# Chunk bounds in four groups over eight places of the array, with the selection turned in 64-column pieces

## The chip, the cores and the metric

The kernel runs on one core of one Trainium2 chip. The metric is the device time of one execution in microseconds (us); the median of the runs stands for a kernel. Names of engines: PE is TensorE (matmuls), ACT is ScalarE, DVE is VectorE, POOL is GpSimd, SP issues most DMAs.

## The reference

Two parts, one after the other. The first is causal attention over 4 batches of 8 heads, 768 positions and 64 dimensions, in which each query sees only 6 of 24 chunks of 32 keys: those with the highest upper bound of the score. The second is a feed-forward block over the 3072 rows of 512 that result.

```python
k_min = np.min(k_chunks, axis=3)
k_max = np.max(k_chunks, axis=3)
ub = np.sum(np.maximum(q[:, :, :, None, :] * k_min[:, :, None, :, :], q[:, :, :, None, :] * k_max[:, :, None, :, :]), axis=-1)
ub = np.where(causal, ub, -1000000000.0)
top_chunks = np.argsort(ub, axis=-1)[..., -top_k:]
scores = scale * np.matmul(q, k.transpose(0, 1, 3, 2))
mask = sel & (pos[:, None] >= pos[None, :])
scores = np.where(mask, scores, -1000000000.0)
attn = softmax(scores); return np.matmul(attn, v)
...
xn = x / rms * rms_g
return (silu(xn @ w_gate) * (xn @ w_val)) @ w_out
```

(The two softmax and silu lines are shortened; the reference writes them out.)

## The kernel before

The work is cut into steps. Each step has the engines that may run it, a modelled duration, a rank, the steps it needs, and the buffers that it opens or uses. Before any instruction is issued, the class `Order` plays the steps through: each engine takes, among the steps that are ready and whose buffers are free, the one with the lowest rank. The steps are then emitted in that order, so this plan fixes the order of the instructions of each engine. A rank is a sum of keys: a time for the place (`a5` for the preparation of pair 5, `l5` for its loads, `s5.0` for its scores, `f1.0` for the first half of batch 1's feed-forward, from the table `TIMES`), an offset for the kind of step in the first or in a later batch (table `RANK`), and a pace times the number of the step.

Attention works in 16 pairs of heads, four to a batch. The preparation of a pair (`prep`) is this chain:

- k and q are loaded by SP and turned by PE (L499) into tiles `kt` and `qt` with two heads of 64 dimensions on 128 partitions and 768 columns; ACT or DVE copies them out of PSUM.
- DVE takes minima and maxima of each chunk (L523, L525). Their difference is the second half of `ku`, and `rt` is the positive part of q, so that the bound is q times the minimum plus rt times the difference.
- PE makes the bounds (L578), as small float32 matmuls: 64 rows (one head) by 32 columns (the chunks) at a place of their own in the array, over 256 queries. There are three groups of 256 queries on three of the four column places, and two heads on the two halves of rows: six places.
- The two results of 96 partitions by 256 columns are copied to `ubs` by ACT or DVE, and turned by PE into `up` (L602, four turns), with queries on the partitions.
- DVE adds the causal mask `cmf` (L610), takes the eight largest of each row (L623, 12 instructions) and compares with the sixth (L631, L636). The result `selq` holds for each of 6 blocks of 128 queries two heads of 64 columns.
- PE turns `selq` into `st` (L647, six turns of 128 by 128), and two copies, one to each head (L315 on ACT, L319 on DVE), bring it into the rows of the operand `qs` that q does not use.

The scores (L712) are matmuls of `ke` with `qs`: 64 rows are k and q, the others a fixed matrix `e_all` and the selection, which adds a large negative number where a chunk is not selected. The rows in use are 89 for one head and 128 for the other. ACT takes the exponential (L729), PE multiplies by v (L748), DVE divides and writes the rows `xb` (L763, L764). Pair 3 is scored in two halves of the queries (`s3.0` and `s3.3`), the others whole.

The feed-forward block runs in halves of a batch, 384 rows each. The rows are normalised and turned (L830); then come 12 steps of gate (L864) and value (L885) matmuls, tanh and two products on ACT and DVE, and the projection (L905) with its store. The feed-forward half `f0.0` needs the first three row blocks of all four pairs of batch 0; the half `f0.1` the other three.

The PSUM banks are eight (`ps`), with limits for each use; three sets of score operands (`set`), two buffers of rows (`xb`).

Of the kernel before, what the change touches and what calls it, by code (L numbers as in the profile page):

```python
# [8 lines left out]
FP32 = mybir.dt.float32  # L9
# [18 lines left out]
        av=-17.99, dif=13.38, eps=15.18, exp=27.56, kC=-0.16, kE=17.53, kT=-23.78, kload=11.87,  # L28
        kmn=22.63, kmx=-12.26, max=-61.12, qC=54.11, qE=9.45, qT=-26.18, qload=3.56,
        relu=19.97, root=46.9, sc=-0.2, sel=-44.38, selC=-65.79, selT=-14.62, sq=17.6, tp=7.31,  # L30
        tpE=23.87, ub=-8.14, ubE=18.31, ubm=-7.93, up=-18.76, vload=-10.11, xb=16.97, xs=25.31,
    ),
    dict(
        av=-15.37, dif=-18.4, eps=-17.61, exp=10.72, gate=-5.25, hh=-22.22, kC=13.17, kE=-4.98,
        kT=-1.03, kload=0.17, kmn=-41.84, kmx=7.41, mask=-29.68, max=20.31, out=-9.4, po=2.14,
        poE=-2.1, qC=3.39, qE=-3.84, qT=-9.81, qload=-3.16, relu=-0.35, root=5.16, sc=-14.52,
        sel=-54.35, selC=-24.54, selT=7.81, sq=37.75, tanh=-21.52, tg=-0.17, tp=-45.38,
        tpE=12.9, ub=-13.71, ubE=24.1, ubm=13.82, up=-10.31, val=1.94, vload=19.85, xb=5.4,
        xs=11.14,
# [3 lines left out]
TIMES = dict(  # L43
    pace0=1.79, pace1=0.05, pacen=0.06, step=0.1, w=-2.85, w0=-2.54, w1=11.0, w2=43.12,
    w3=21.59,
)
for p, x in enumerate((
    13.52, 22.61, 22.24, 36.48, 50.85, 112.1, 73.87, -93.04, 37.77, 179.84, 214.26, 206.91,
    226.56, 220.49, 246.48, 309.33,
)):  # L50
    TIMES[f"a{p}"] = x
for p, x in enumerate((
    -126.16, -42.1, -31.16, -25.49, -5.8, -2.4, 25.7, 37.05, 124.03, 155.87, 181.98, 170.69,
    131.44, 202.23, 282.06, 292.24,
)):
    TIMES[f"l{p}"] = x
for p, x in enumerate((
    -21.19, 10.14, 25.24, 47.31, 25.73, 45.99, 41.69, 141.19, 75.77, 129.26, 185.37, 166.25,
    277.81, 251.34, 143.95, 194.34,
)):  # L60
    TIMES[f"s{p}.0"] = x
for p, x in enumerate((
    101.79,
), 3):
    TIMES[f"s{p}.3"] = x
for i, x in enumerate((
    -27.88, 91.19, 93.6, 105.43, 90.44, 106.14, 282.0, 341.37,
)):
    TIMES[f"n{i // 2}.{i % 2}"] = x
for i, x in enumerate((  # L70
    50.8, 120.12, 121.42, 191.74, 229.9, 291.93, 266.48, 339.66,
)):
    TIMES[f"f{i // 2}.{i % 2}"] = x
for i, x in enumerate((
    2.53, 0.58, 0.91, 2.16, 0.75, 2.5, 0.51, 0.73,
)):
    TIMES[f"pacef{i // 2}.{i % 2}"] = x

# [141 lines left out]
def kernel(  # L224
# [24 lines left out]
    KM = D + NCH + 1  # L249
    W = S // 2  # L250
    G = 3
# [82 lines left out]
    SELQ = [const.tile([P, NT, 2, D], BF16, name=f"selq{i}") for i in range(SLOTS["selq"])]  # L334
    VX = [const.tile([P, 2 * NT, D + 1], BF16, name=f"vx{i}") for i in range(SLOTS["vext"])]
    e_all = const.tile([D, S], BF16, name="e_all")
    cmf = const.tile([P, NT, 2, NCH], FP32, name="cmf")
# [9 lines left out]
    def make_ident(e):  # L347
# [13 lines left out]
        VX[i][:, :, D:D + 1], 1.0)) for i in range(SLOTS["vext"])]  # L361

    def e_step(n):
        if n == 0:
            nc.gpsimd.memset(e_all[:], -BIGE)
        elif n == 1:
            nc.gpsimd.affine_select(
                out=e_all[:], in_=e_all[:], compare_op=ALU.is_ge, fill=0.0,
                base=0, pattern=[[1, S]], channel_multiplier=-CH,
            )  # L370
        elif n == 2:
            nc.gpsimd.affine_select(
                out=e_all[:], in_=e_all[:], compare_op=ALU.is_ge, fill=0.0,
                base=CH - 1, pattern=[[-1, S]], channel_multiplier=CH,
            )
        else:

            nc.gpsimd.affine_select(
                out=e_all[:], in_=e_all[:], compare_op=ALU.not_equal, fill=-1.0,
                base=-NCH, pattern=[[0, S]], channel_multiplier=1,  # L380
            )
# [4 lines left out]
    c_e = prev  # L386
# [11 lines left out]
    def make_cmf(n):  # L398
        if n == 0:
            nc.gpsimd.memset(cmf[:], 0.0)  # L400
        for g4 in (2 * n, 2 * n + 1):
            nc.gpsimd.affine_select(
                out=cmf[32 * g4:32 * (g4 + 1)], in_=cmf[32 * g4:32 * (g4 + 1)],
                compare_op=ALU.is_ge, fill=-BIGC,
                base=g4, pattern=[[4, NT], [0, 2], [-1, NCH]], channel_multiplier=0,
            )

    c_cm = add("cmf", "POOL", 1.5, -70, lambda e: make_cmf(0), [c_e])
    c_cm = add("cmf", "POOL", 1.1, -69, lambda e: make_cmf(1), [c_cm])

# [60 lines left out]
    def prep(c, i0, nb, at, lr):  # L471
# [96 lines left out]
        nj = nq // P  # L568
# [3 lines left out]
        def bounds(e):  # L572
            t = [tile_of(x, [P, 2 * P], FP32, "ub") for x in ub]
            for m, src in ((0, big["q"].tile), (1, rel.tile)):
                for g in range(G):
                    for h in range(2):
                        rows = slice(h * D, (h + 1) * D)
                        nc.tensor.matmul(  # L578
                            t[h][g * CH:(g + 1) * CH, 0:nq], KU[c.ku.slot][rows, m, :],
                            src[rows, g * nq:(g + 1) * nq],  # L580
                            start=(m == 0), stop=(m == 1), tile_position=(h * D, g * CH))

        um = add("ub", "PE", 0.25 + 0.8 * nq / 256, rank(at, b, "ub"), bounds,
# [3 lines left out]
        for h in range(2):  # L587
            def ub_out(e, h=h):
                if ubs.tile is None:
                    tile_of(ubs, [G * CH, 2, 2 * P], FP32, "ubs")  # L590
                evict(e, ubs.tile[:, h, 0:nq], ub[h].tile[0:G * CH, 0:nq])

            ue.append(add("ubE", "", {e: {"ACT": act(nq), "DVE": dve(nq)}[e] for e in BOUNDS},
                          rank(at, b, "ubE", h, "step"), ub_out, [um], opens=[ubs],
                          uses=[ub[h]]))
        up, ubm, m8 = Buf("ps", "prep"), Buf("ubm"), Buf("small")

        def up_turn(e):
            t = tile_of(up, [P, G, nj, 2, CH], FP32, "up")
            for j in range(nj):  # L600
                for h in range(2):
                    nc.tensor.transpose(  # L602
                        t[:, :, j, 1 - h, :], ubs.tile[:, h, j * P:(j + 1) * P],
                        ident_f[0:G * CH, 0:G * CH])

        ut = add("up", "PE", 0.083 * 2 * nj, rank(at, b, "up"), up_turn, ue, opens=[up], uses=[ubs])

        def causal(e):
            t = tile_of(ubm, [P, NT, 2, NCH], FP32, "ubm")
            nc.vector.tensor_tensor(  # L610
                out=t[:, 0:nb].rearrange("p i h c -> p (i h) c"),
                in0=up.tile[:].rearrange("p g j h c -> p (g j h) c")[:, :, 0:NCH],
                in1=cmf[:, i0:i0 + nb].rearrange("p i h c -> p (i h) c"), op=ALU.add)
# [3 lines left out]
        for j in range(0, nb, 3):  # L617
            def top(e, j=j):
                if m8.tile is None:
                    tile_of(m8, [P, NT, 2, 8], FP32, "m8")  # L620
                for x in range(j, j + 3):
                    for h in range(2):
                        nc.vector.max(out=m8.tile[:, x, h, :], in_=ubm.tile[:, x, h, :])  # L623
# [4 lines left out]
        def pick(e):  # L628
            s12 = SELQ[sq.slot][:, 0:nb].rearrange("p i h e -> p (i h) e")
            m12 = m8.tile[:, 0:nb].rearrange("p i h e -> p (i h) e")  # L630
            nc.vector.scalar_tensor_tensor(  # L631
                out=s12[:, :, 0:NCH],
                in0=m12[:, :, 5:6].to_broadcast([P, 2 * nb, NCH]),
                scalar=THRFLOOR, in1=ubm.tile[:, 0:nb].rearrange("p i h e -> p (i h) e"),
                op0=ALU.max, op1=ALU.is_gt)
            nc.vector.tensor_scalar(  # L636
                out=s12[:, :, NCH:NCH + 1], in0=m12[:, :, 0:1], scalar1=-GUARD,
# [6 lines left out]
        def sel_turn(e):  # L644
            t = tile_of(st, [P, nb * P], BF16, "st")
            for j in range(nb):
                nc.tensor.transpose(  # L647
                    t[:, j * P:(j + 1) * P], SELQ[sq.slot][:, j].rearrange("p h c -> p (h c)"),
                    ident_b[:])

        sT = add("selT", "PE", nb * 0.057, rank(at, b, "selT"), sel_turn, [pk, c_idb], opens=[st], uses=[sq])
        fin = []
        for hl, rows in ((0, slice(D, P)), (1, slice(0, D))):
            def sel_out(e, hl=hl, rows=rows):
                evict(e, QS[c.set.slot][hl][rows, cols], st.tile[rows, :])

            fin.append(add("selC", "", {"DVE": dve(n / 2), "ACT": act(n)},
                           rank(at, b, "selC", hl, "step"), sel_out, [sT],
# [28 lines left out]
    def scores(c, i0, nb, at, pace, adds):  # L687
# [3 lines left out]
        for hl in range(2):  # L691
            kk = slice(0, KM) if hl == 0 else slice(0, P)
# [4 lines left out]
            for g, (nd, regions) in enumerate(groups):  # L697
# [25 lines left out]
                need = list(c.sel) + [y for z in c.ke.values() for y in z] + [c_tri] + c_ke  # L723
# [244 lines left out]
```

## Time and profile before

| what | value |
|---|---|
| median of 3 runs | 330.02 us (328.67 to 330.77) |
| span of the profiled execution | 461.2 us |
| mean granted TensorE clock in it | 0.663 |
| busy: PE, DVE, ACT, POOL | 446.6, 246.5, 214.3, 118.0 us |
| moved by DMA | 27.89 MB, mean 60 GB/s |

The profiled execution is known by its span alone: no time outside the span is recorded for it. It was taken at a lower granted TensorE clock than full speed, and it is longer than each of the runs in the first row. A busy PE is one with a matmul under way; matmuls overlap, and their ends are modelled. Rows of the profile name line, engine, operation, written and read tiles, shapes and count, then busy time and the mean duration of one instruction in ns, then the idle time of the engine before them with what ended it. Rows of the timeline begin with the start and the duration in us, from the first instruction to the last of those merged.

### The profile page before, as it was taken

What the parts mean: (1) busy time and instruction counts of PE and PEld (TensorE: products, weight loads), DVE (VectorE), ACT (ScalarE), POOL (GpSimd) and SP (SyncE); (2) the same over time, 40 slices, a digit from 0 to 9 for tenths busy, and PEclk for the clock granted to TensorE, in tenths of its full rate; (3) what the DMA queues carried; (4) which work ended last, traced back from release to release, by engine and by line L of the source; (5) the groups of instructions that cost most, each with busy time, mean ns of one, the idle gap of its engine ahead of it and who ended that gap; (6) DMA issues with size and microseconds to landing.
All of it is one profiled execution on the core that took longest, in us unless ns stands there. A gap on an engine that the chain in (4) does not pass through costs nothing.

```text
span 461.2 us, 7853 instructions
## 1 busy us (share of the span) xinstructions
PE 446.6 (97%) x2978; PEld 253.4 (55%) x2996; DVE 246.5 (53%) x663; ACT 214.3 (46%) x448; POOL 118.0 (26%) x172
## 2 busy tenths in 40 slices
PE   3999999999999999999999999999999999999996
PEld 2677754665666555435666664654565644534442
DVE  2977776665465735404767564367046465603520
ACT  3777772463556643114656684630473634123201
POOL 7755342314442420002552453200110110000000
PEclk9666666666666666666666666666666666666666
DMA  9999769248848250003430203100100000011002
GB/s 186 210 207 143 104 105 100 41 47 53 185 89 134 18 112 9 0 30 105 111 36 1 18 2 46 41 1 1 47 24 0 2 0 1 1 63 52 0 0 91
DMA packets 82645, 27.89 MB, mean 60 GB/s; under 512 B 75568, under 2 KB 79408, under 8 KB 82608
## 3 DMA queue, kind: packets, MB, share of 16 engines
q1 hardware_dynamic: 52528, 19.14, 17.9%
q0 software_dynamic: 28512, 7.87, 17.3%
q10 hardware_dynamic: 1568, 0.39, 0.5%
q8 instruction: 23, 0.38, 0.3%
q14 instruction: 14, 0.11, 0.1%
HBM read 28.57 MB, written 6.29 MB: 76 GB/s over the span
## 4 chain that ended last, share of the span: by engine, by line
PE 96%; DMA 2%; ACT 1%; issue 1%; ACTq 0%
PE vp L885 20%; PE gp L864 20%; PE po L905 20%; PE sc L712 12%; PE av L748 6%; PE ub L578 5%; PE pk L499 3%; PE pq L499 3%; PE tp L830 2%; PE up L602 2%; PE st L647 2%; DMA knat<-in_k_dram 1%; PE sc L718 1%; DMA qnat<-in_q_dram 1%; ACT pt L729 0%
## 5 line engine op out<-in xcount | busy, mean ns | idle before, releaser
L885 PE MATMUL vp<-xT,wv 128*128 128x384 bf16 x384 | 107.5, 430 | 0.0
L864 PE MATMUL gp<-xT,wg 128*128 128x384 bf16 x384 | 107.3, 430 | 0.0
L729 ACT ACTIVATE pt<-sc 128x512 bf16<-128x512 f32 x192 | 91.1, 551 | 20.5 <-PE sc L712 16.6
L905 PE MATMUL po<-wo,hh 128*128 128x512 bf16 x274 | 97.8, 513 | 1.9 <-issue 0.8
L871 ACT ACTIVATE sg<-gp 128x384 bf16<-128x384 f32 x96 | 47.1, 491 | 88.9 <-PE gp L864 78.9
L877 DVE SCALAR_TENSOR_TENSOR tg<-sg,gp 128x384 bf16<-128x384 bf16 x96 | 52.5, 550 | 52.2 <-ACT sg L871 51.4
L893 DVE TENSOR_TENSOR hh<-vp,tg 128x384 bf16<-128x384 f32 x96 | 53.1, 555 | 38.1 <-PE vp L885 37.9
L712 PE MATMUL sc<-qs,ke 89*128 89x128 bf16 (+5 forms) x416 | 72.1, 309 | 0.4 <-PE sc L712 0.2
L885 PEld LDWEIGHTS <-wv 128*128 128x128 bf16 x384 | 45.3, 120 | 43.7 <-issue 3.4
L864 PEld LDWEIGHTS <-wg 128*128 128x128 bf16 x384 | 45.1, 120 | 41.4 <-issue 2.5
L905 PEld LDWEIGHTS <-hh 128*128 128x128 bf16 x288 | 33.5, 120 | 46.8 <-issue 43.8
L735 POOL TENSOR_SCALAR_AFFINE_SELECT pt<-pt 128x512 bf16<-128x512 bf16 (+1 forms) x48 | 24.8, 532 | 102.1 <-ACT pt L729 100.5
L748 PEld LDWEIGHTS <-pt 128*128 128x128 bf16 x672 | 39.1, 111 | 16.5 <-issue 8.2
L712 PEld LDWEIGHTS <-ke 89*128 89x128 bf16 (+1 forms) x420 | 38.2, 116 | 16.0 <-issue 8.6
L748 PE MATMUL av<-vx,pt 128*128 128x65 bf16 x672 | 45.2, 217 | 0.3 <-ACT pt L729 0.2
L317 ACT ACTIVATE osb<-po 128x512 f32<-128x512 f32 x23 | 13.7, 597 | 64.5 <-PE po L905 64.5
L319 POOL CAST ke<-kt 64x768 bf16<-64x768 f32 x31 | 26.1, 843 | 61.0 <-ACT kt L315 57.5
L319 POOL CAST qs<-qt 64x768 bf16<-64x768 f32 x31 | 29.0, 936 | 49.1 <-ACT qt L315 32.5
L499 PE MATMUL pq<-ident_f,qnat 128*128 128x128 f32 x96 | 20.4, 358 | 5.2 <-DMA qnat<-in_q_dram 5.2
L499 PE MATMUL pk<-ident_f,knat 128*128 128x128 f32 x96 | 21.7, 354 | 2.7 <-DMA knat<-in_k_dram 2.5
L525 DVE TENSOR_REDUCE ku<-kt 128x24 f32<-128x768 f32 x16 | 15.1, 945 | 12.7 <-ACT kt L315 12.6
L820 DVE SCALAR_TENSOR_TENSOR xs<-xb,ri,gains 128x512 bf16<-128x512 bf16 x24 | 17.3, 758 | 7.8 <-PE tp L830 5.2
(70 smaller groups left out, 366.7 us busy)
## 6 DMA issues: line engine op xcount, KB each, us to landing
out_dram<-osb SPq DMA_DIRECT2D x24, 256.0 KB, 2.0
qnat<-in_q_dram SPq DMA_DIRECT2D x31, 192.0 KB, 4.8
knat<-in_k_dram SPq DMA_DIRECT2D x31, 192.0 KB, 4.5
vx<-in_v_dram POOLq DMA_DIRECT2D x16, 192.0 KB, 4.7
wv<-in_moe_w_val_dram POOLq DMA_DIRECT2D x2, 768.0 KB, 7.9
wg<-in_moe_w_gate_dram POOLq DMA_DIRECT2D x2, 768.0 KB, 7.0
wo<-in_moe_w_out_dram POOLq DMA_DIRECT2D x2, 768.0 KB, 7.6
ke<-e_all SPq DMA_DIRECT2D x4, 96.0 KB, 3.5
```

The source lines that it names most:

```text
L319: engine[e].tensor_copy(out_, in_)
L499: nc.tensor.transpose(t[:, j * P:(j + 1) * P], nat[w].tile[:, j0 + j].rearrange("p h d -> p (h d)"), ident_f[:])
L712: nc.tensor.matmul(t[:, x:x + m, :].rearrange("p a b -> p (a b)"), ke[kk, kb * P:(kb + 1) * P], qs[kk, q0 * P:(q0 + m) * P], start=not tri ...
L729: nc.scalar.activation(out=t[:, 0:nn, :], in_=sc.tile[:, 0:nn, :], func=ACT.Exp, scale=SCALE)
L735: nc.gpsimd.affine_select(out=pt.tile[:, 0:nd, :], in_=pt.tile[:, 0:nd, :], compare_op=ALU.is_ge, fill=0.0, base=0, pattern=[[0, nd], [1, ...
L748: nc.tensor.matmul(av.tile[:, qi - i0, :], pt.tile[:, x, :], VX[c.v.slot][:, hl * NT + kb, :], start=(begin and m == 0), stop=(left[0] == ...
L864: nc.tensor.matmul(t[:], wg[:, g, hs], XT[b].tile[:, g, cols], start=(g == 0), stop=(g == NP - 1))
L871: nc.scalar.activation(out=t[:], in_=gp.tile[:], func=ACT.Tanh, scale=0.5)
L877: nc.vector.scalar_tensor_tensor(out=t[:], in0=sg.tile[:], scalar=1.0, in1=gp.tile[:], op0=ALU.add, op1=ALU.mult)
L885: nc.tensor.matmul(t[:], wv[:, g, hs], XT[b].tile[:, g, cols], start=(g == 0), stop=(g == NP - 1))
L893: nc.vector.tensor_tensor(out=t[:], in0=vp.tile[:], in1=tg.tile[:], op=ALU.mult)
L905: nc.tensor.matmul(po.tile[:], hhs[ht].tile[:, th * P:(th + 1) * P], wo[:, ht, :], start=(ht == 0), stop=(ht == NHT - 1))
```

## The change

The bounds are made in four groups of 192 queries, so that two heads take all eight places (two halves of rows, four columns). Both results have 128 partitions by 192 columns. Three turns of 128 by 128 bring queries on the partitions, and the row of a partition block is now a third of the 384 columns of two heads. `selq` holds 3 blocks by 4 groups by 32 columns. It is turned in eight pieces of 64 columns, two groups at a time, one to each half of the columns of the array; one block goes to both halves, since 192 is one and a half blocks. The copies to `qs` are four instead of two, each for 32 partitions and two stretches of 192 queries. The rows of the selection now differ by group, so `qs` is filled with zeros beforehand (`qs0`), `e_all` stands twice (`e2`), and both heads contract over all 128 rows. `cmf` is built with eight selects of smaller pieces. All the numbers in `RANK` and `TIMES` are new.

```diff
-        relu=19.97, root=46.9, sc=-0.2, sel=-44.38, selC=-65.79, selT=-14.62, sq=17.6, tp=7.31,
+        qload=-55.01, relu=59.39, root=126.02, sc=-68.74, sel=-202.87, selC=-132.4, selT=-15.25,
...
-for p, x in enumerate((
-    101.79,
-), 3):
-    TIMES[f"s{p}.3"] = x
+    13.12, "step": 3.34, "w": 21.12, "w0": 25.23, "w1": 31.28, "w2": 104.4, "w3": 102.34,
+    442.18, "s14.0": 295.15, "s15.0": 68.82, "s2.0": 85.92, "s3.0": -76.29, "s3.3": 358.03,
...
-    KM = D + NCH + 1
     W = S // 2
-    G = 3
+    G = 4
+    NU = 3
...
+    c_qz = []
+    for i in range(NB):
+        for hl, rows in ((0, slice(D, P)), (1, slice(0, D))):
+            c_qz.append(add("qs0", "DVE", 0.38, -85 + 2 * i + hl, lambda e, i=i, hl=hl, rows=rows: nc.vector.memset(
+                QS[i][hl][rows, :], 0.0)))
...
-    c_e = prev
+    c_e = add("e2", "DVE", 0.55, -55, lambda e: nc.vector.tensor_copy(e_all[CH:2 * CH, :], e_all[0:CH, :]),
+              [prev])
...
         def up_turn(e):
-            t = tile_of(up, [P, G, nj, 2, CH], FP32, "up")
-            for j in range(nj):
-                for h in range(2):
-                    nc.tensor.transpose(
-                        t[:, :, j, 1 - h, :], ubs.tile[:, h, j * P:(j + 1) * P],
-                        ident_f[0:G * CH, 0:G * CH])
+            t = tile_of(up, [P, NU, G, CH], FP32, "up")
+            flat = ubs.tile[:].rearrange("p h q -> p (h q)")
+            for u in range(NU):
+                x = NU - 1 - u
+                nc.tensor.transpose(t[:, u].rearrange("p g c -> p (g c)"),
+                                    flat[:, x * P:(x + 1) * P], ident_f[:])
...
         def sel_turn(e):
-            t = tile_of(st, [P, nb * P], BF16, "st")
-            for j in range(nb):
-                nc.tensor.transpose(
-                    t[:, j * P:(j + 1) * P], SELQ[sq.slot][:, j].rearrange("p h c -> p (h c)"),
-                    ident_b[:])
+            t = tile_of(st, [P, G // 2, 2, P], BF16, "st")
+            for g2 in range(G // 2):
+                for m in range(2):
+                    for side in range(2):
+                        u = 1 - m + side
+                        nc.tensor.transpose(
+                            t[side * D:(side + 1) * D, g2, m],
+                            SELQ[sq.slot][:, u, 2 * g2:2 * g2 + 2].rearrange("p g c -> p (g c)"),
+                            ident_b[:], tile_position=(0, side * D))
...
-        for hl, rows in ((0, slice(D, P)), (1, slice(0, D))):
-            def sel_out(e, hl=hl, rows=rows):
-                evict(e, QS[c.set.slot][hl][rows, cols], st.tile[rows, :])
+        for m, (hl, r) in enumerate(((0, 0), (1, 0), (0, 1), (1, 1))):
+            rows = slice((1 - hl) * D + r * CH, (1 - hl) * D + (r + 1) * CH)
+            x0 = D * hl
+
+            def sel_out(e, hl=hl, r=r, x0=x0, rows=rows):
+                evict(e, QS[c.set.slot][hl][rows, :].rearrange("p (g r i) -> p g r i", r=2, i=nq)[:, :, r, :],
+                      st.tile[rows].rearrange("p g m n -> p g (m n)")[:, :, x0:x0 + nq])
...
-            kk = slice(0, KM) if hl == 0 else slice(0, P)
+            kk = slice(0, P)
```

The keys of the table that the prediction adds up, before and after: `f0.0` 50.8 and 24.8, with pace 2.53 and 1.78 and the offset of gate -5.25 and -1.18; `s4.0` 25.73 and 72.37, `s5.0` 45.99 and 78.51, `s7.0` 141.19 and 103.21, `s6.0` 41.69 and 187.88, with the offset of sc in later batches -14.52 and -40.89; `s3.3` 101.79 and 358.03, with that of the first batch -0.2 and -68.74. The loads go by `l4` to `l15` and the offsets of kload and qload.

125 lines of the change are left out of this document (47 added, 78 removed), and 12 rows, old and new, of the table TIMES.

## The prediction

> **What bounds the kernel now.** I read the page first: span, shares, clock, chain.
>
> ```profile
> span 461.2 us, 7853 instructions
> PE 446.6 (97%) x2978; PEld 253.4 (55%) x2996; DVE 246.5 (53%) x663; ACT 214.3 (46%) x448; POOL 118.0 (26%) x172
> ...
> PEclk9666666666666666666666666666666666666666
> ...
> PE 96%; DMA 2%; ACT 1%; issue 1%; ACTq 0%
> PE vp L885 20%; PE gp L864 20%; PE po L905 20%; PE sc L712 12%; PE av L748 6%; PE ub L578 5%; PE pk L499 3%; PE pq L499 3%; PE tp L830 2%; PE up L602 2%; PE st L647 2%; DMA knat<-in_k_dram 1%; PE sc L718 1%; DMA qnat<-in_q_dram 1%; ACT pt L729 0%
> ```
>
> In this execution TensorE is the whole chain, and it ran at about two thirds of its clock from the second slice on. The timed executions were faster: 330.02 us median against a span of 461.2. So the profile's stages must be read at another clock. The second view is a table of stretches, cut where the feed-forward matmuls come and go.
>
> ```profile
> core 0: us, PE busy (x) PEld busy (x) DVE busy (x) ACT busy (x) POOL busy (x), PEclk, DMA share, GB/s
> 0.00:12.00 12.00, 4.24 (x19) 3.88 (x20) 3.76 (x11) 4.92 (x8) 8.64 (x24) 1.00 1.04 187
> 12.00:63.00 51.00, 50.60 (x567) 35.49 (x566) 40.52 (x136) 38.76 (x86) 27.35 (x35) 0.66 1.09 165
> 63.00:119.00 56.00, 55.68 (x358) 32.80 (x359) 35.33 (x96) 24.76 (x52) 18.89 (x23) 0.65 0.58 63
> 119.00:161.00 42.00, 41.44 (x343) 25.05 (x346) 26.66 (x77) 25.58 (x53) 14.44 (x22) 0.65 0.65 108
> 161.00:228.00 67.00, 66.63 (x312) 34.51 (x314) 27.91 (x61) 22.11 (x43) 10.64 (x13) 0.65 0.25 60
> 228.00:290.00 62.00, 61.47 (x532) 37.68 (x533) 38.62 (x117) 38.70 (x86) 27.08 (x40) 0.65 0.21 26
> 290.00:329.00 39.00, 38.88 (x203) 20.22 (x202) 21.05 (x53) 14.07 (x28) 3.33 (x4) 0.65 0.04 14
> 329.00:363.00 34.00, 33.82 (x283) 20.57 (x282) 14.84 (x43) 20.68 (x43) 5.98 (x12) 0.65 0.05 17
> 363.00:461.00 98.00, 93.79 (x381) 43.26 (x383) 37.84 (x73) 24.75 (x52) 1.71 (x2) 0.65 0.07 25
> ```
>
> Multiplied by the granted clock (PE busy times 0.65 or 0.66), TensorE's work from 12 to 461 us is 33.4, 36.2, 26.9, 43.3, 40.0, 25.3, 22.0 and 61.0 us, together 288; with the first 12 us that is 300. So 330 us can be read in two ways: (a) the timed runs had the full clock and TensorE stood idle for 30 us, or (b) it was nearly always busy at a mean clock of 288/318 = 0.91. Nothing shown decides between them. Under (a) the other engines matter: in the stretch 12 to 63, attention without feed-forward work, VectorE's 40.5 and ScalarE's 38.8 us exceed TensorE's 33.4, so VectorE binds, by 7.1 us; in 119 to 161 and 228 to 290 they are almost level. Putting the larger number in each stretch gives 307, and the 4 us at the end in which TensorE has no more work make 311; the other 19 us would be waits, which the order of the work decides.
>
> **The change part by part.** I work in the profile's units and convert at the end. Bounds and turns first: a pair of heads that stands between other TensorE work.
>
> ```profile
> 107.52 0.41 PE L748 MATMUL av<-vx,pt 128*128 128x65 bf16 x6
> 107.86 0.43 PE L578 MATMUL ub<-qt,ku 64*32 64x256 f32 x6
> ...
> 108.77 0.53 PE L578 MATMUL ub<-rt,ku 64*32 64x256 f32 x6
> 109.23 0.39 PE L905 MATMUL po<-wo,hh 128*128 128x512 bf16 x1
> ...
> 110.46 0.63 PE L602 MATMUL up<-ident_f,ubs 96*128 96x96 f32 x4
> ...
> 116.82 0.70 PE L647 MATMUL st<-ident_b,selq 128*128 128x128 bf16 x6
> ...
> 17.77 1.15 PE L499 MATMUL pq<-ident_f,qnat 128*128 128x128 f32 x6
> L578 PE MATMUL ub<-rt,ku 64*32 64x256 f32 x192 | 14.1, 515 | 0.0
> ```
>
> *ub.* 192 records over 16 pairs are 12 for each of the two sources: six matmuls, each in two parts, and the six places start together. The first round starts at 107.86, the fourth and last at 108.77: 0.91 us for three rounds, 0.30 each at a granted 0.65, about 512 cycles of 2.4 GHz x 0.65 (0.33 us). So places do run side by side, and a round costs its columns only. Eight places of 192 columns are again four rounds, a quarter shorter: 4 x 0.33 x 0.25 = -0.33 us a pair, -5.2 us over 16.
>
> *The toll of a change of form.* From the last ub round to the next matmul are 109.23 - 108.77 = 0.46 us where the stream is 0.33: about 0.13 on leaving. Before the first round the previous av matmul, a stream of 0.04 us, can be placed by its end (107.52 + 0.41 = 107.93, some 0.20 after its start) at about 107.74, so 0.08 on entering. Together 0.21 us for going to the small places and back. It is paid at ub before and after.
>
> *up.* Four turns of 96 columns become three of 128. Four take 0.63, less a tail of 0.20 about 0.11 each; six of 128 float32 columns (the pq row) take 1.15, so (1.15 - 0.20)/6 = 0.16 each, three 0.48 against 0.43: +0.05 a pair, +0.8.
>
> *selT.* Six full turns take 0.70 - 0.20 = 0.50, 0.083 each. Now there are eight of 64 columns, in two column halves. No row of before shows this form. Bounds: paired without a toll, 4 x 0.083 = 0.33, -0.17 a pair (-2.7); not paired and with the toll, 8 x 0.083 + 0.21 = 0.87, +0.37 a pair (+5.9). I take paired with ub's toll, 0.33 + 0.21 = 0.54, +0.04 (+0.6), because ub, the nearest row, shows both.
>
> The Trainium skill, on the page TensorEngine Tiling (Array Packing), under Tiling Modes, says that changing the tiling mode, not merely the tile, drains the engine. By that rule selT gains a drain that the full-size turns had not; with the drain the sum of TensorE is the -3.8 below, without it -7.1. ub's 0.21 us agrees with the rule; no run here shows it yet for 64-column pieces.
>
> TensorE's sum: -5.2 + 0.8 + 0.6 = **-3.8 us** at the profile's clock (bounds -7.1 and +1.5), -2.5 at the full one. In an execution as throttled as this one the span would become 457.4, since TensorE is full there.
>
> *Copies.* These run on ScalarE and VectorE, whose times do not follow TensorE's clock.
>
> ```profile
> L315 ACT ACTIVATE qs<-st 64x768 bf16<-64x768 bf16 x16 | 12.9, 806 | 11.4 <-PE st L647 7.3 <-DVE qs L319 4.0
> L319 DVE COPY qs<-st 64x768 bf16<-64x768 bf16 x16 | 8.9, 553 | 20.1 <-ACT qs L315 13.0 <-PE st L647 7.0
> L315 ACT ACTIVATE ubs<-ub 96x256 f32<-96x256 f32 x22 | 7.7, 379 | 15.2 <-PE ub L578 15.2
> L319 DVE COPY ubs<-ub 96x256 f32<-96x256 f32 x10 | 4.1, 418 | 6.4 <-PE ub L578 6.4
> L729 ACT ACTIVATE pt<-sc 128x512 bf16<-128x512 f32 x158 | 84.5, 605 | 17.6 <-PE sc L712 13.9 <-PE av L748 1.8 <-POOL qs L319 0.9
> L729 ACT ACTIVATE pt<-sc 128x128 bf16<-128x128 f32 x30 | 8.5, 285 | 2.9 <-PE sc L712 2.7
> ```
>
> ScalarE's price of a column is (605 - 285)/384 = 0.83 ns. ubs loses 64 columns: 53 ns on ScalarE; on VectorE, if 0.27 us of the 418 ns are the columns, 67. 22 x 53 + 10 x 67 = -1.8 us. The selection's two copies of 768 become four of 384: ScalarE 806 - 320 = 486 each, VectorE 553 less half of some 400 = 350 each. Two on each engine cost 1.67 us against 1.36, +0.31 a pair, +5.0 over 16. If VectorE kept 553 for the smaller, split copy it would be +6.5 more; if halves were free of fixed cost, 1.36, no change. I take +5.0. Net +3.2 over two engines, 1.6 each.
>
> *Scores* contract over 128 rows for both heads instead of 89 and 128.
>
> ```profile
> L712 PE MATMUL sc<-qs,ke 128*128 128x128 bf16 x162 | 22.7, 262 | 0.0
> L712 PE MATMUL sc<-qs,ke 89*128 89x128 bf16 x162 | 22.0, 266 | 0.0
> ```
>
> Rows cost nothing. The sums, the eights of maxima and the thresholds keep their counts and elements: nothing.
>
> *Start.* Six zero fills of QS, the second copy of e_all and eight causal selects in place of four.
>
> ```profile
> L358 DVE MEMSET selq<- 128x384 uint32 x3 | 1.1, 378 | 0.1
> 5.33 0.51 DVE L391 COPY ke<-e_all 64x768 bf16<-64x768 bf16 x1 [2.88 <-POOL e_all L378]
> 5.85 0.56 DVE L392 COPY ke<-e_all 64x768 bf16<-64x768 bf16 x1
> 7.29 0.56 DVE L560 TENSOR_SCALAR rt<-qt 128x768 f32<-128x768 f32 x1 [0.87 <-ACT qt L315]
> 8.48 1.09 POOL L402 TENSOR_SCALAR_AFFINE_SELECT cmf<-cmf 32x288 f32<-32x288 f32 x2
> 11.48 0.83 POOL L319 CAST ke<-kt 64x768 bf16<-64x768 f32 x1 [1.91 <-ACT kt L315]
> ```
>
> 6 x 0.38 = 2.3 us fit in VectorE's 2.88 us of waiting, the copy's 0.5 in its 0.87, the selects' extra (under 0.6 us each time) in GpSimd's 1.91. Nothing; without that cover at most 3 us, on VectorE alone.
>
> *Order.* Every rank is new, so every queue is, SP's loads included (pairs 4, 5, 7, 8, 6, 12 and on, where it was 4 to 8 in turn). Adding the diff's keys: the first feed-forward half gets gate ranks 25 to 65 (were 48 to 104), level with the scores of pairs 4 and 5 (31 to 42) rather than behind them (11 and 31); the second half of pair 3, which feed-forward half 0.1 needs, goes from 102 to 289. Bounds: the 19 us of waits found under (a), to either side. I choose -2.6, a seventh of them: earlier feed-forward work gives TensorE something beside attention, the stretch that VectorE binds; this is the term with the least behind it.
>
> Conversion: under (a) the saving counts where TensorE binds. Of 16 pairs some 6 are prepared before 63 us, so -2.5 x 10/16 = -1.6, and the copies add about half of their 1.6, +0.8: -0.8. Under (b), -3.8 x 0.65/0.91 = -2.7. Middle -1.7: 330.0 - 1.7 = 328.3; with the order **325.7 us**.
>
> **The rivals.** *The order gives nothing*: 328.3. For it: the steps and what each needs stay the same, and under (b) no order can help. Against: so many keys moved.
>
> *The late half of pair 3* (slower). With rank 289 it stands behind the scores of pairs 4 to 7 (31 to 152) on TensorE, and half 0.1 cannot start without it. If batch 1's attention then runs without feed-forward matmuls beside it, that stretch is bound like 12 to 63, 7.1 us lost over about four pairs: 328.3 + 7.1 = 335.4. It decides from about 5 us, some three of the four pairs. For it: the rank. Against: half 0.0 still gives TensorE 24 gate and value steps, and the sets of operands are three.
>
> *Pieces that do not pair and copies that do not shrink* (slower; the change then doesn't do what it says). TensorE +1.5, at full clock +1.0; copies 5.0 + 6.5 - 1.8 = 9.7, 4.8 on each engine, half of it binding, +2.4: 333.4. For it: no row shows the form. Against: ub's places start together, and ScalarE's price goes by columns.
>
> **How the numbers follow.** Forecast 0.45, order gives nothing 0.25, late half 0.18, no pairing 0.12. About 1% (3.3 us) is what a measurement here can tell from no change: faster 0.45, same 0.25, slower 0.30. The range goes down to 317, where the order takes back half of the waits, and up to 336, which holds the slower rivals. The forecast's own range is 317 to 326.7.
>
> **What would show it.** The changed profile should have four ub rounds of about 0.25 us; selT records in two starts together, with about 0.13 us lost after the last; three up turns of about 0.16; four copies a pair near 486 and 350 ns. TensorE's busy time times clock should fall by 2 to 3 us. Wrong: selT starts 0.083 apart eight times, copies that stay at 800 and 550, or a stretch past the first feed-forward half with no gp, vp or po in it.

## The result: slower by 1.4%

The changed kernel takes 334.26 us (median of 4 runs, 332.86 to 334.38), the kernel before 329.35 on the same chip (328.56 to 330.77). The ratio is 1.0136, with an interval of 1.0101 to 1.0171. The forecast was 325.7 us, faster. Two of the four runs before lie near 328.6 us and two above 330 (see The slow windows); against the 328.6 to 328.8 us that this kernel takes as a median in all the experiments below, the loss is some 5.5 us.

The profiled execution after has a span of 331.1 us and a time of its own of 332.86. Its page:

```profile
span 331.1 us, 8195 instructions
PE 311.5 (94%) x3140; PEld 200.7 (61%) x3140; DVE 246.1 (74%) x688; ACT 209.1 (63%) x466; POOL 116.5 (35%) x172
...
PEclk9989999999999999999999999999999999999999
...
PE 85%; ACT 6%; DVE 4%; DMA 2%; issue 1%; POOL 0%; ACTq 0%; DVEq 0%
```

The clock digits are 9 but for one 8: this is the full clock but for one short dip, where the execution profiled before was granted two thirds of it. The two pages can't be compared line by line. So the kernel before was run again unchanged (e1), and that profile had the full clock too. What e1 was expected to show:

> The kernel before, unchanged, to have its profile at the clock of the kernel after (0.995). Theory 1 (the new work costs): the streams of TensorE for bounds and turns, start to start, are shorter here than after, so that the difference of some 4 to 5 us lies in these groups and in the copies. Theory 2 (the new order costs): bounds and turns take about 1 to 3 us more here than after, and TensorE's waits are some 5 to 7 us shorter.

It took 328.53 us. Its page, and under it both kernels in three stretches (attention without feed-forward work is the middle one):

```profile
span 326.8 us, 7853 instructions
PE 309.9 (95%) x2978; PEld 200.4 (61%) x2996; DVE 242.3 (74%) x663; ACT 206.1 (63%) x448; POOL 119.3 (36%) x172
```

```profile
0.00:12.00 12.00, 4.92 (x22) 4.56 (x23) 4.53 (x12) 5.60 (x10) 8.76 (x24) 1.00 1.09 191
12.00:63.00 51.00, 47.08 (x625) 32.71 (x624) 48.19 (x160) 42.36 (x96) 32.34 (x40) 1.00 1.20 174
63.00:300.00 237.00, 234.91 (x2212) 151.07 (x2228) 178.62 (x472) 151.68 (x332) 78.16 (x109) 1.00 0.38 65
```

The same stretches after:

```profile
0.00:12.00 12.00, 4.76 (x23) 4.39 (x24) 6.56 (x19) 5.43 (x9) 8.66 (x27) 1.00 1.09 187
12.00:63.00 51.00, 44.33 (x653) 32.37 (x652) 43.85 (x160) 42.29 (x99) 29.55 (x38) 0.97 1.24 195
63.00:300.00 237.00, 235.07 (x2330) 150.54 (x2328) 188.46 (x497) 154.74 (x349) 78.27 (x108) 1.00 0.37 58
```

The first number after the length is TensorE's busy time. The span grew by 4.3 us: TensorE is idle for 2.7 us more (331.1 - 311.5 against 326.8 - 309.9) and busy for 1.6 more. All of the new idle time lies between 12 and 63 us (47.08 to 44.33, 2.75 less); from 63 to 300 both are full. The busy time hides a slow clock, which the granted 0.97 of the middle stretch shows. In windows of the length of the dip, after:

```profile
11.55:14.96 3.41, 1.58 (x39) 0.86 (x37) 3.21 (x6) 2.24 (x5) 1.83 (x3) 1.00 1.07 221
14.96:18.37 3.41, 3.41 (x28) 3.06 (x15) 2.09 (x4) 1.35 (x4) 3.00 (x5) 0.50 0.97 206
```

For 3.41 us the clock is halved, so what TensorE does there takes up to 1.7 us longer. Without that its busy time would be about as before: of the saving of 2.5 us that was forecast at full clock, nothing is seen in this sum.

### The profile page after: what moved, and what is told of

Its sections match the earlier page's. It is cut to its first block, busy times and chain, and to the rows that moved or that the text cites. A ratio compares the mean times of both kernels' runs of the same rounds, so it can differ in the third digit from the quotient of the medians.

```text
span 331.1 us, 8195 instructions
## 1 busy us (share of the span) xinstructions
PE 311.5 (94%) x3140; PEld 200.7 (61%) x3140; DVE 246.1 (74%) x688; ACT 209.1 (63%) x466; POOL 116.5 (35%) x172
## 4 chain that ended last, share of the span: by engine, by line
PE 85%; ACT 6%; DVE 4%; DMA 2%; issue 1%; POOL 0%; ACTq 0%; DVEq 0%
PE gp L852 19%; PE vp L873 19%; PE po L893 18%; PE sc L700 10%; PE av L736 5%; ACT pt L717 3%; PE pq L484 3%; PE ub L562 3%; PE pk L484 3%; ACT qs L292 2%; PE tp L818 2%; PE up L587 2%; PE st L630 1%; DMA knat<-in_k_dram 1%; DVE qs L296 1%
## 5 line engine op out<-in xcount | busy, mean ns | idle before, releaser
L717 ACT ACTIVATE pt<-sc 128x512 bf16<-128x512 f32 (+1 forms) x192 | 89.5, 582 | 4.6 <-PE av L736 2.3
L873 PE MATMUL vp<-xT,wv 128*128 128x384 bf16 x384 | 74.7, 326 | 0.0
L852 PE MATMUL gp<-xT,wg 128*128 128x384 bf16 x384 | 74.3, 326 | 0.2 <-ACT qs L292 0.2
L893 PE MATMUL po<-wo,hh 128*128 128x512 bf16 x288 | 68.7, 379 | 0.0
L700 PE MATMUL sc<-qs,ke 128*128 128x128 bf16 (+2 forms) x420 | 55.2, 251 | 1.8 <-DVE qs L296 0.7
L873 PEld LDWEIGHTS <-wv 128*128 128x128 bf16 x384 | 36.1, 98 | 21.6 <-issue 0.3
L700 PEld LDWEIGHTS <-ke 128*128 128x128 bf16 x420 | 30.6, 98 | 13.8 <-issue 3.2
L292 ACT ACTIVATE qs<-st 32x384 bf16<-32x384 bf16 x33 | 15.9, 482 | 19.8 <-PE st L630 10.6
L450 POOL DMA_DIRECT2D vx<-in_v_dram x16 | 17.0, 1068 | 9.6 <-PE av L736 7.5
L296 DVE COPY qs<-st 32x384 bf16<-32x384 bf16 x31 | 11.0, 354 | 12.0 <-ACT qs L292 10.8
```

The source lines that it names most:

```text
L296: engine[e].tensor_copy(out_, in_)
L700: nc.tensor.matmul(t[:, x:x + m, :].rearrange("p a b -> p (a b)"), ke[kk, kb * P:(kb + 1) * P], qs[kk, q0 * P:(q0 + m) * P], start=not tri ...
L717: nc.scalar.activation(out=t[:, 0:nn, :], in_=sc.tile[:, 0:nn, :], func=ACT.Exp, scale=SCALE)
L852: nc.tensor.matmul(t[:], wg[:, g, hs], XT[b].tile[:, g, cols], start=(g == 0), stop=(g == NP - 1))
L873: nc.tensor.matmul(t[:], wv[:, g, hs], XT[b].tile[:, g, cols], start=(g == 0), stop=(g == NP - 1))
L893: nc.tensor.matmul(po.tile[:], hhs[ht].tile[:, th * P:(th + 1) * P], wo[:, ht, :], start=(ht == 0), stop=(ht == NHT - 1))
```

## The experiments

Each was compared with the kernel before on the same chip, which took 328.6 to 328.8 us there (medians); a difference in us is that of the two medians. "Old" and "new" stand for the kernels before and after.

**Work or order?** e2 does the new work in the old plan's order, e3 the old work in the new plan's order.

```diff
  e2, in each of the two old steps selC
-  evict(e, QS[..][hl][rows, cols], st.tile[rows, :])
+  for r in range(2): evict(e, QS[..][hl][rows of r], st.tile[rows of r])  # 32 x 384
  e3, in the new four steps selC
+  if r == 0: evict(e, QS[..][hl][rows, cols], st.tile[rows, :])           # 64 x 768
```

> The work of after (four groups, eight places, 64-column pieces, 128 rows) in exactly the order of before: the two copies of one head go to the engine that had its one copy. Theory 1 (the work costs): 333 to 335 us, as after. Theory 2 (the order costs): 326 to 329.5, at or below before.

> The work of before (three groups, six full turns, two copies) in exactly the order of after: copies on the engines that have the first two of the four there, the other two steps empty. Theory 1 (the work costs): 328 to 331, at most a little above before. Theory 2 (the order costs): 334 to 338, above after by what the new bounds save.

e2: 334.97 us, 1.0172 (1.0143 to 1.0201), +6.4 us. e3: 332.03, 1.0087 (1.0054 to 1.0120), +3.4. So the new work alone loses all that the change loses, whereas the new order costs the old work 0.9% and yet doesn't add to the loss of the new work. The middle stretch shows both, e2 first, then e3:

```profile
12.00:63.00 51.00, 44.38 (x658) 31.91 (x658) 46.62 (x154) 42.48 (x100) 29.79 (x38) 0.97 1.12 170
```

```profile
12.00:63.00 51.00, 45.36 (x595) 32.52 (x594) 43.03 (x148) 40.03 (x91) 29.66 (x37) 0.97 1.23 194
```

**Which part of the work?** Five kernels put one or two parts into the old kernel.

```diff
  e4, more copies
+  for r in range(2): x = slice(r * W, (r + 1) * W); evict(e, QS[..][hl][rows, x], st.tile[rows, x])
  e5, bounds and turns up alone: G = 4, the new bounds, ub_out and up_turn; selection as before
  e6, 64-column pieces: twelve in place of six full turns
+  for side in range(2): transpose(t[side * D:(side + 1) * D, j * P:(j + 1) * P],
+                                  SELQ[..][:, j, side, :], ident_b[:], tile_position=(0, side * D))
  e7, rows and fills
-  kk = slice(0, KM) if hl == 0 else slice(0, P)
+  kk = slice(0, P)          # and six fills of QS with zeros
  e10: e6 and e4 together
```

> Before, with each of the two copies of the selection cut into two copies of 384 columns on the same engine; all else, the order too, as before. Copies of 384 columns took 482 ns (ScalarE) and 354 (VectorE) after, against 806 and 553 for 768, so a pair pays some 0.16 us more on each engine, 2.5 us on each over 16 pairs. Theory 1 (the form of the selection eats the gain of the bounds): +1 to +2.5 us. Theory 2 (the bounds themselves cost, by more records and a chain that waits for eight places): within 0.7 us of before.

> Before, with the new bounds (four groups of 192) and the three new turns alone; the selection keeps its two copies and six full turns and works on the same number of elements, but for other queries than the masks belong to, so the output is not the reference's. Theory 1: -1.5 to -3 us, since the bounds' streams fell from 16.9 to 14.7 us between the two profiles in the old order. Theory 2: 0 to +2 us.

> Before, with each of the six full turns of the selection replaced by two 64-column pieces in the two column halves, twelve pieces in six rounds: the same columns streamed, the same result, and only the form of the array changes. Theory 1: the change of form costs about 0.10 us on entering and 0.10 on leaving, 0.19 a pair, 3 us on TensorE, of which 2 to 3 show. Theory 2: within 0.7 us of before.

> Before, with scores over 128 rows for both heads and the six zero fills at the start. Theories 1 and 2: within 0.5 us of before. A third theory, that the start pays for the fills: +1 us or more, with the first score matmul that much later.

> Before, with twelve 64-column pieces and each copy in two, both as in the runs that had one of them; the bounds as before, the same result. Costs that add up: 1.8 + 1.5, 331.5 to 332.3. If pieces and copies raise each other's price: 333 or more.

| kernel | us | difference | ratio (interval) |
|---|---|---|---|
| e4 | 330.12 | +1.4 | 1.0037 (1.0015 to 1.0059) |
| e5 | 327.46 | -1.2 | 0.9951 (0.9933 to 0.9969) |
| e6 | 330.44 | +1.8 | 1.0048 (1.0027 to 1.0070) |
| e7 | 328.61 | -0.1 | 1.0001 (0.9981 to 1.0020) |
| e10 | 331.64 | +2.9 | 1.0084 (1.0062 to 1.0106) |

The bounds gain 1.2 us, pieces and copies lose 1.8 and 1.4 and add up in e10, rows and fills cost nothing. Together that is some +2 us at most (e6 has twelve pieces where the new kernel has eight; see Pieces below), and e2 lost 6.4. Something of the new work was in none of them.

**What is left.** e9 is e2 with six full turns in place of the pieces. e12 and e13 go for the shape of the copies: e4 cut them by columns, with 64 partitions each, while the new kernel cuts them into groups of 32 partitions and two stretches of 192 columns. e12 puts that shape into the old kernel; e13 is e2 with e4's shape. All three leave out part of the result: e12 copies half of the selection, e9 and e13 copy columns that do not belong to the queries; only their times count.

```diff
  e12, old kernel with zero fills and scores over 128 rows, for r in range(2)
+  evict(e, QS[..][hl][rows of r].rearrange("p (g r i) -> p g r i", r=2, i=192)[:, :, r, :], st.tile[rows of r])
  e13, e2 with copies of 64 partitions, for r in range(2)
-  evict(e, QS[..][hl][rows of r], st.tile[rows of r])
+  evict(e, QS[..][hl][rows, r * W:(r + 1) * W], flat[rows, r * P:r * P + W])
```

> The new work in the order of before, but with six full turns of the selection in place of the eight pieces; bounds and the four copies as in the run that had all the new work in the old order. The turned blocks are not those that the copies need and the mask is weak (30 in place of 30000), so the output is not the reference's. Costs that add up: copies +1.5 and bounds -1.1, 328.6 to 329.5. If the saving of the bounds is lost where VectorE and ScalarE, now with longer copies, are waited for: 330 to 331.5.

> Before, with zero fills and with the two copies of a pair replaced by four of the new shape (32 partitions, two stretches of 192 columns), on the engines that have them in the new work in the old order; bounds and turns as before. Half of the selection is not copied, so the output is not the reference's. In the traces two copies of one engine take 0.86 us with 64 partitions and 0.96 with 32, and the chain of a pair's copies 1.53 and 1.76 us, before 1.39. Theory 1 (the chain of copies, split by partitions, carries most of the loss): 331.5 to 333. Theory 2 (copies cost as the contiguous ones did, and something else in the new work is missing from the account): 329.8 to 330.6.

> All the new work in the old order, but each of the four copies takes 64 partitions and 384 columns in one stretch, the shape of the four copies that cost 1.5 us; same number of elements for each engine's time, but the columns are not those that belong, and the mask is weak (30 in place of 30000), so the output is not the reference's. Theory 1: 1.5 to 3 us faster than with the new shape (333.6 at full clock), 330.5 to 332. Theory 2: 333 to 334.

e9: 334.79 us, 1.0181 (1.0155 to 1.0207); without the pieces the loss stays. e12: 336.18, 1.0197 (1.0163 to 1.0230), +7.4 us, where e4 lost 1.4 with as many copies of as many columns and twice the partitions. e13: 328.83, 0.9992 (0.9970 to 1.0013): with another shape of the copies the whole loss of e2, 6.1 us between the two, is gone, although the rest of the new work, the pieces too, is in it. **The shape of the copies is the cause**, shown in both directions. It is worth more than was expected in either: e9 and e12 came out some 3 us above their expectations, e13 1.7 us below. (With e6's twelve pieces the single parts add up to +1.9 us, with the 0.2 us that the new kernel's eight cost, by the reading under Pieces below, to +0.3; e13's +0.1 agrees with the second sum.)

The rows of the copies, e4, e12, and the new kernel:

```profile
L315 ACT ACTIVATE qs<-st 64x384 bf16<-64x384 bf16 x32 | 13.8, 479 | 7.0 <-PE st L647 3.7 <-DVE qs L319 2.9 <-PE pq L499 0.3
L319 DVE COPY qs<-st 64x384 bf16<-64x384 bf16 x32 | 9.9, 349 | 8.9 <-ACT qs L315 6.1 <-PE st L647 1.5 <-PE vp L887 0.7
```

```profile
L315 ACT ACTIVATE qs<-st 32x384 bf16<-32x384 bf16 x32 | 15.4, 481 | 8.8 <-PE st L649 3.9 <-DVE qs L319 3.1 <-PE pk L501 0.9
L319 DVE COPY qs<-st 32x384 bf16<-32x384 bf16 x32 | 11.3, 352 | 10.3 <-ACT qs L315 7.9 <-PE st L649 1.2 <-PE pk L501 0.8
```

```profile
L292 ACT ACTIVATE qs<-st 32x384 bf16<-32x384 bf16 x33 | 15.9, 482 | 19.8 <-PE st L630 10.6 <-DVE qs L296 9.0
L296 DVE COPY qs<-st 32x384 bf16<-32x384 bf16 x31 | 11.0, 354 | 12.0 <-ACT qs L292 10.8 <-PE vp L873 0.7 <-PE st L630 0.2
```

One copy lasts the same in e4 and e12 (479 and 481, 349 and 352 ns). But 32 of 479 ns are busy for 13.8 us, less than 32 x 479 = 15.3: two copies in a row overlap by 0.1 us. With 32-partition groups 32 of 481 make 15.4: they don't overlap. The copies of e12 also go in two stretches of columns. That the groups alone are enough to part them is seen in e14 (below), where one engine makes both copies of a pair, each in one stretch, the second starting at another group of 32 partitions than the first:

```profile
L315 ACT ACTIVATE qs<-st 64x768 bf16<-64x768 bf16 x22 | 17.7, 804 | 4.1 <-PE st L647 3.7
L319 DVE COPY qs<-st 64x768 bf16<-64x768 bf16 x10 | 5.6, 555 | 1.6 <-PE st L647 1.4
```

Here too 22 x 804 = 17.7 and 10 x 555 = 5.6, with no overlap. The first pair in e12:

```profile
19.48 0.51 PE L649 MATMUL st<-ident_b,selq 128*128 128x128 bf16 x6 [0.47 <-DVE selq L638]
20.02 0.99 ACT L315 ACTIVATE qs<-st 32x384 bf16<-32x384 bf16 x2 [0.78 <-PE st L649]
20.56 0.22 PE L717 MATMUL sc<-qs,ke 128*128 128x128 bf16 x1
...
21.04 0.87 ACT L315 ACTIVATE kt<-pk 128x384 f32<-128x384 f32 x2
21.05 0.71 DVE L319 COPY qs<-st 32x384 bf16<-32x384 bf16 x2 [0.82 <-ACT qs L315]
21.07 0.33 PE L717 MATMUL sc<-qs,ke 128*128 128x128 bf16 x3 [0.29 <-ACT qs L315]
```

and in e13:

```profile
18.66 0.41 PE L650 MATMUL st<-ident_b,selq 128*64 128x128 bf16 x8 [0.58 <-DVE selq L636]
19.11 0.86 ACT L315 ACTIVATE qs<-st 64x384 bf16<-64x384 bf16 x2 [0.83 <-PE st L650]
19.71 0.53 PE L718 MATMUL sc<-qs,ke 128*128 128x128 bf16 x4
20.00 0.87 ACT L315 ACTIVATE kt<-pk 128x384 f32<-128x384 f32 x2
20.01 0.61 DVE L319 COPY qs<-st 64x384 bf16<-64x384 bf16 x2 [0.31 <-ACT qs L315]
```

Two things differ. Two copies take 0.99 and 0.71 us in e12, 0.86 and 0.61 in e13. And the first four scores of a head take 128 queries each. In e13 the first copy brings the first 384 queries, so three scores start from 19.71 on, 0.6 us after it began, and the fourth at 20.03, behind the second copy (the row merges the four). In e12 the two copies bring every other stretch of 192 queries; the second score needs both, and three of the four wait until 21.07, when both copies of the head are done. From the starts and ends of all 16 pairs, the copies of a pair last 1.39 us in the old kernel, 1.53 in e4 and e13, 1.75 in e12, 1.76 in e2 and 1.77 in the new one. In all of them VectorE's copies wait for ScalarE's, or the other way: the copies of one `st` tile follow each other over both engines. What stands behind a copy in the queue of its engine waits too, as `kt` on ScalarE does in both views. The 0.22 us between the two shapes are 3.5 us over 16 pairs, less than the 6.1 between e2 and e13. How the loss splits between the lost overlap, the scores' wait for both copies and the work queued behind was not settled; no run changes the groups of partitions and the stretches of queries one at a time.

The rule for VectorE stands in the Trainium skill, page VectorE: DVE Perf Modes, section Two Vector instructions with no wait between them: an instruction whose input or output starts in another group of 32 partitions than the one before is held until the earlier ones have finished. The trace agrees on VectorE (0.71 us for two of 352 ns held, 0.61 for two of 349 not held), and ScalarE's 0.99 and 0.86 us show the same, and so does e14 on both engines, though the page speaks of VectorE.

**Fewer changes of engine.** In the new order the four copies of a pair often change engine from one to the next. Waits of a copy for the other engine's copy (us in all, times, longest), old kernel in e1, then new:

```profile
DVE qs L319 <- ACT qs L315: 6.8, 11, 1.0
ACT qs L315 <- DVE qs L319: 2.5, 5, 1.2
```

```profile
DVE qs L296 <- ACT qs L292: 10.8, 15, 2.0
ACT qs L292 <- DVE qs L296: 9.0, 17, 1.2
```

16 waits became 32, 9.3 us became 19.8. e8 and e14 give all copies of a pair to the engine of the first, in the new and the old kernel; e16 gives each head's pieces a PSUM tile of their own, in the kernel of e15 (below).

```diff
  e8 and e14, in sel_out
+  if c.copier is None: c.copier = e
+  e = c.copier
  e16, on top of e15
+  st = [Buf("ps", "prep") for _ in range(2)]     # a piece goes to t[side], a copy reads st[1 - hl]
```

> After, with all four copies of a pair on the engine that has the first of them; the order is kept. Copies out of one PSUM tile are taken in turn, and after shows 32 waits of one engine's copy for the other's (19.8 us) where before has 16 (9.3 us). Theory 1 (hand-overs between the engines hold up both queues): 1 to 3 us faster than after, 331.5 to 333. Theory 2 (length of the copies and toll of the pieces alone): as after or slower, 334 to 336, since one engine gets the whole load.

> Before, with both copies of a pair on the engine of the first, the order kept. If the hand-over between the engines costs here as it did after (1.7 us less there with one engine): 327.3 to 328.3, below before. If the second engine was a relief: 329 to 331.

> The same, but the pieces of the two heads go to a PSUM tile each, so that the copies of one head need not wait for those of the other; the plan has one more PSUM tile to place for each pair. If the waits between the engines carry the cost: 1.5 to 4 us faster than the run with one tile. If the two copies of one head in series and the later start of the scores carry it: within 1 us of it. Below 328.7 it would be faster than before and after.

e8: 332.52 us, 1.0104 (1.0083 to 1.0126), 1.7 us less than the new kernel. e14: 331.70, 1.0072 (1.0050 to 1.0094), +2.9 against the old kernel. So one engine is no gain as such. Where it gains, in the new order, handing the copies to and fro is the likely cost, some 1.7 us (no run of e8 is as slow as the fastest of the new kernel, but the intervals of the two ratios overlap, and the copies of a pair last 1.80 us, no less than before). In e8's rows the waits of one copy for another have gone:

```profile
L292 ACT ACTIVATE qs<-st 32x384 bf16<-32x384 bf16 x40 | 19.3, 482 | 11.3 <-PE st L630 10.6
L296 DVE COPY qs<-st 32x384 bf16<-32x384 bf16 x24 | 8.5, 354 | 2.4 <-PE st L630 1.8
```

e16: 338.49, 1.0279 (1.0250 to 1.0309), 4 us less than e15. Its plan came out otherwise than e15's, so this points to the waits and doesn't prove them.

**The ranks.** e15 is the new kernel with the old `RANK` and `TIMES`, its plan made anew.

> After, with the tables of before: the plan is made again from the old ranks and the new durations. Theory 1 (the new copies are what costs, and the new order makes up for part of it): 333 to 336, no better than after. Theory 2 (the new order is what costs): at or below 330.

342.52 us, 1.0391 (1.0351 to 1.0431): 8 us above the new kernel and above what either account expected. The new ranks suit the new work far better than the old ranks do, and still don't make up for its copies.

**The slow windows.** e11 puts 30 idle matmuls between the halves of the first pair's bounds, to keep TensorE busy ahead of the dip.

```diff
+  for _ in range(30 if m == 1 and p == 0 else 0):
+      nc.tensor.matmul(t[0][:, 256:384], ident_b[:], ident_b[:], start=False, stop=False)
```

> After, with 30 idle matmuls of 128 columns between the two halves of the first pair's bounds, where TensorE waited 2.1 us for the difference of the chunks; they add to columns that nobody reads. Theory 1 (the waits at the start let the granted clock fall to half for one window of 3.4 us in every run of after, and that costs 1.4 to 2 us): the clock goes from 0.994 to 0.998 or more in most runs, and the time to about 332.5. Theory 2 (the clock's dip is hidden by other engines): 334, as after.

334.26 us, 1.0156 (1.0132 to 1.0181): nothing gained, but the dip only moved, to 22.8 us in its trace, so this left its price open. What precedes a dip can be read: after, 1.58 us busy of 3.41 came ahead of the window at 0.50. In e2 it was

```profile
49.49:52.90 3.41, 2.17 (x32) 1.19 (x30) 3.23 (x14) 3.41 (x9) 1.09 (x3) 1.00 1.09 187
52.90:56.31 3.41, 3.33 (x51) 2.45 (x52) 3.15 (x7) 2.70 (x7) 0.79 (x2) 0.50 0.82 103
```

and the old kernel (e1) has no dip there with somewhat more to do:

```profile
46.20:49.60 3.40, 2.64 (x41) 1.85 (x38) 3.19 (x22) 3.40 (x10) 0.07 (x1) 1.00 0.83 108
49.60:53.00 3.40, 2.79 (x53) 1.70 (x50) 3.30 (x7) 3.02 (x7) 1.88 (x3) 1.00 1.05 150
```

The busy share alone does not decide it: after, TensorE was busy for 2.15 us of the 3.41 from 21.79 on, as little as in e2 ahead of the dip, and the next window had the full clock. So what brings the dip stays open.

Its price can be estimated from the runs of the old kernel: nearly all those at a mean clock of 0.998 or more took 328.5 to 328.8 us, those at 0.994 or 0.995, about a third, 329.7 to 331.2. All four runs of the new kernel were at 0.993 to 0.995, and of e2's six the one at 0.999 was the fastest, 333.6 us. So, by this estimate, 1 to 2.5 us of the new kernel's loss lie in a dip ahead of which TensorE had idle time, and e2's one run without it still lost 5.0. e9 and e12 lost 6 and 7 at clocks of 0.993 to 1.0, most of their runs at 0.997 or more: the copies cost this without a dip.

The Trainium skill, page TensorE: Matmul & The Clock Gate, Part 1, says that the clock is either full or half and is decided over free-running windows of about 3.4 us, idle windows bringing the half. The 0.50 over 3.41 us agrees; the windows ahead of it were not idle, but 46 and 64% busy. The 0.65 that the profile before shows throughout, as a mean, is neither full nor half, and no run here explains it.

## Why the prediction was wrong, point by point

**The two readings.** Reading (a) was right: full clock, but TensorE idle for 16.9 us of the span (e1) where 30 were counted; 1.7 of the 30 lie outside the span (328.53 against 326.8), and busy time did not shrink with the clock as assumed (309.9 us, not 300). That VectorE binds from 12 to 63 us was half right: there it has 48.19 us in e1, but TensorE has 47.08, so the two are level and not 7.1 us apart; the stretch of the slowed execution had other work in it.

**Bounds.** Right, with a smaller gain. The timelines of one pair after:

```profile
154.54 0.56 PE L562 MATMUL ub<-qt,ku 64*32 64x192 f32 x16
154.89 0.53 PE L562 MATMUL ub<-rt,ku 64*32 64x192 f32 x16
155.36 0.66 PE L852 MATMUL gp<-xT,wg 128*128 128x384 bf16 x3
...
165.10 0.41 PE L630 MATMUL st<-ident_b,selq 128*64 128x128 bf16 x8
165.44 0.82 PE L893 MATMUL po<-wo,hh 128*128 128x512 bf16 x3
```

and before, in e1:

```profile
244.90 0.65 PE L578 MATMUL ub<-qt,ku 64*32 64x256 f32 x12
245.36 0.62 PE L578 MATMUL ub<-rt,ku 64*32 64x256 f32 x12
245.91 0.46 PE L748 MATMUL av<-vx,pt 128*128 128x65 bf16 x9
...
253.94 0.50 PE L647 MATMUL st<-ident_b,selq 128*128 128x128 bf16 x6
254.27 0.49 PE L885 MATMUL vp<-xT,wv 128*128 128x384 bf16 x2
```

From the first start to the next matmul ub takes 0.82 us where it took 1.01: -0.19 a pair, 3.0 over 16 (3.4 forecast at full clock). In the time, e5 (bounds and turns up alone) shows 1.2.

**Pieces.** They pair in their starts: 0.34 us to the next matmul for eight, 0.33 for six full turns. As medians over the pairs these are 0.347 (after) and 0.335 (e1), some +0.2 us over 16 where +0.6 was forecast, and e2, with the pieces, and e9, without them, differ by 0.2 us. So this term was right, and both sides of it show. In e6, whose twelve pieces stream as many columns as the six turns, 0.459 us pass to the next matmul: a toll of 0.12 us a pair, 2.0 over 16, of which e6 lost 1.8. (The forecast had 0.21 a pair at the profile's clock, 0.14 at the full one.) The new kernel's eight pieces save about as much in columns as they pay in toll. The Trainium skill (TensorEngine Tiling (Array Packing), Tiling Modes) says that a change of the tiling mode drains the engine; e6's loss agrees, 0.11 us a pair that the columns, as many as before when two pieces run at once, do not explain.

**Copies.** This is the step that failed. Their durations were right (486 and 350 forecast, 482 and 354 measured), and so was "two on each engine", +5.0 us over both. But they were costed as busy time, of which half binds: +0.8 net of what the smaller `ubs` copies save. In fact they stand on the way from the selection to the scores, one behind the other. The price is not how long they are busy but when the last of them ends, and that hangs on which partitions and which queries each brings. e4, with the assumed number and durations, lost 1.4 us; the shape that the diff really has lost 7.4 (e12). The term was +0.8 and should have been some 5 to 7 (5 from e2's one run at full clock, 6.1 between e2 and e13, 7.4 in e12). With -1.2 for the bounds and +0.2 for the pieces, e12's 7.4 makes the 6.4 that e2 lost, as closely by luck, since most of e2's runs have a dip and most of e12's have none.

**Rows, fills and start.** Zero, as forecast (e7).

**Order.** The -2.6 had the least behind it. With the old work the new order costs 3.4 us (e3), of which part goes with dips: its two runs at full clock took 329.90 and 330.72. With the new work the two orders differ by less than the intervals tell (1.0136 against 1.0172), and against a plan from the old ranks the new one is worth 8 us. The value of an order belongs to the work that it was searched for.

**The rivals.** The late half of pair 3 named the right sign and nearly the size (335.4), but not the cause: from 63 to 300 us TensorE is busy for 235.07 of 237, so no half started late. The rival of pieces and copies (333.4) was nearest in time; its place, the copies, was right, its mechanism not: they shrank, and pieces paired.

## What to carry to other kernels

Cost a copy that stands between two matmuls by when its consumer can start: which slice of it the consumer reads, and what is queued behind it. When one copy must become several, let them start at the same partitions, and let the first bring in one stretch what the consumer takes first (here the first 384 queries), as e13 does. A new layout that saves time on one engine should be tried with its copies in the old shape (e13) before its gain is counted.

## What the hardware showed that was not expected

Two copies in a row on one engine overlapped by about 0.1 us when they used the same partitions (e4, e13), and not at all when the second started at another group of 32 (e2, e12, e14); this held on both engines. A window of 3.41 us in which TensorE was busy for 1.58 or 2.17 us was followed by one at half clock; others with 2.15 and, in e1, 2.64 and 2.79 were not, so the busy share does not settle it. And going to the 64-column pieces and back costs some 0.11 us a pair (1.8 us over 16 in e6), although the pieces start two at a time: in most pairs of the new kernel at 0, 3, 80, 83, 136, 139, 192 and 195 ns.
